# Loading float32 q and k with several tokens per row, and turning them head by head into stepped columns

## The chip, the core and the metric

The kernel runs on one core of a Trainium2 chip. The metric is the device time of one execution in microseconds. The core's engines work side by side, each through its own list of instructions in order: PE (matmuls, with its weight loads shown apart as PEld), DVE (vector), ACT (activation), POOL and SP. SP issues all DMAs here; they run on sixteen DMA engines.

## The reference

Attention with a decay, for 8 batches, 8 heads, 576 tokens and a head size of 64, followed by a feed-forward layer over all 4608 tokens:

```python
scores = scale * np.matmul(q, k.transpose(0, 1, 3, 2))
cum = np.cumsum(np.log(np.clip(f, 0.0001, 1.0)), axis=-1)
decay = cum[:, :, :, None] - cum[:, :, None, :]
scores = np.where(causal, -1000000000.0, scores + decay)
scores = scores - np.max(scores, axis=-1, keepdims=True)
attn = np.exp(scores)
attn = attn / (np.sum(attn, axis=-1, keepdims=True) + 1e-09)
out = np.matmul(attn, v)
...
h = x @ w_in          # x: out as (4608, 512); w_in: 512 x 2048
g = np.where(h >= 1, h, np.where(h <= -1, 0.0, (h + 1) ** 2 / 4))
return g @ w_out      # 2048 x 512
```

## The kernel before

Attention is cut into jobs. A job is one batch, one pair of heads and a range of blocks of 128 tokens (r0 to r1; the fifth block has 64 tokens). Batch 0 is cut in two, so jobs 0 to 3 are the four head pairs with token blocks 0 and 1, jobs 4 to 7 the same pairs with blocks 2 to 4 as queries and all five as keys; each later batch gives four jobs of five blocks. Jobs 0 to 11 (`NQK = 12`) compute q times k in float32; the later ones split q and k into two float16 parts and turn them with DMA transposes. Jobs 0 to 4 (`NPE = 5`) also keep the rest of attention in float32 on PE (`turn_rows`, L513 and L519, turns the probabilities; `early_values`, L544, multiplies them with v); from job 5 on the probabilities are split on ACT and DVE (L589, L595) and turned by DMA transposes (pT, L601 and L604).

`load` (L351, L355) fetches q and k of a job into one of two tiles, qk32_0 and qk32_1 (shown as qk_0 and qk_1), three jobs ahead. `early_prepare` turns them on PE (L388) into PSUM and copies them with ACT (L389) into a tile that has head size on the partitions and tokens along the row. `load_decay` (L362) loads a row of the running decay sums, cum_d, broadcast to all partitions, into one of three buffers called ck, once per job and head; a buffer is free again when POOL has used it for all token blocks of that head. `scores` multiplies q and k (L482) and lets POOL make the decay part from ck (L488) with its causal mask (L492); DVE adds the two and takes the minimum (L571), ACT takes the exponential (L575). The decay sums are computed at the start (f loaded, a scan on DVE, written to cum_d at L163).

The feed-forward weights are float32 blocks of 1024 KB, loaded by L201 into place (or into the tiles early and x1, shown as x) and then split: DVE turns the bits of each (L211, L214, L217), ACT takes the norm (L221) and the high part (L225), POOL (L227, L228) or DVE (L230) the low part. How many blocks are split in which job is set by the tables CONVERT and LOADS. When the first eight are done, DVE makes the scales early_z for the first units of the feed-forward layer, whose matmuls are L657 and L685. Units of it fill PE between the steps of attention, by a quota per job.

The order of the instructions on each engine isn't that of the source: a list scheduler orders them when the program is built, by its own model of when each is ready. A change of one part therefore moves others. SP too has one fixed order, and each DMA there also waits for the one issued eight DMAs earlier, whose semaphore it takes over.

Of the kernel before, what the change touches and what calls it, by code (L numbers as in the profile page):

```python
# [15 lines left out]
P = 128  # L16
# [15 lines left out]
NQK = 12  # L32
# [13 lines left out]
def kernel(  # L46
# [19 lines left out]
    nc = tc.nc  # L66

    B, H, S, D = q.shape
    DM, DF = w_in.shape
    NPAIR = H // 2  # L70
    NT5 = -(-S // P)
    LAST = NT5 - 1
    FULL = LAST * P
# [8 lines left out]
    ncut = NPAIR * sum(len(c) for c in CUTS.values())  # L82
# [60 lines left out]
    ident = const.tile([P, P], F32, name="ident")  # L143
# [186 lines left out]
    def load(ji):  # L330
        w = Pair()
        w.b, w.hp, w.r0, w.r1 = jobs[ji]
        w.p = ji
        w.sds = {}
        w.s0, w.s1 = P * w.r0, min(P * w.r1, S)
        w.cuts = [(w.s0, w.s1)] if w.s1 - w.s0 <= 512 else [(0, 64), (64, S)]
        h0 = 2 * w.hp
        flat = qk32[ji % 2].rearrange("p j h t d -> p (j h t d)")
        w.x32 = []
        for j, src in enumerate((q, k)):  # L340
            s_ = src[w.b, h0:h0 + 2]
            t0 = 0 if j else w.r0
            nt = w.r1 - t0
            x = flat[:, j * 2 * NT5 * D:j * 2 * NT5 * D + 2 * nt * D]
            w.x32.append(x)
            dst = x.rearrange("p (t h d) -> p h t d", t=nt, h=2)
            if NQK <= ji < max(NQK, ncut) + 2 and w.r1 == NT5:
                nc.gpsimd.memset(dst[64:P, :, nt - 1, :], 0.0)
            full = min(w.r1, LAST)
            for hh in range(2):  # L350
                nc.sync.dma_start(  # L351
                    dst[:, hh, 0:full - t0, :], s_[hh, P * t0:P * full, :].rearrange("(t p) d -> p t d", p=P)
                )
            if w.r1 == NT5:
                nc.sync.dma_start(dst[0:64, :, nt - 1, :], s_[:, FULL:S, :].rearrange("h p d -> p h d"))  # L355
        w.ck = []
        return w
# [17 lines left out]
    def early_prepare(w):  # L375

        t_ = early_qk[(w.p + NQK) % 2]
        w.nsig, w.nalpha = -8.0, -0.125
        bh = w.b * H + 2 * w.hp
        w.cqs = cq[:, :, bh:bh + 2]  # L380
        w.terms = ((t_[:, 0], t_[:, 1]),)
        for j in range(2):
            pt = ps.tile([P, 1024], F32, name="s")
            t0 = 0 if j else w.r0
            n = w.s1 - P * t0
            for c0 in range(0, n, P):
                m = min(P, n - c0)
                nc.tensor.transpose(pt[:, c0:c0 + m], w.x32[j][0:m, c0:c0 + P], ident[0:m, 0:m])  # L388
            nc.scalar.activation(t_[:, j, 0:n], pt[:, 0:n], AF.Copy)  # L389

    def measure(w):
# [17 lines left out]
    def prepare(w):  # L409
        if w.p < NQK:  # L410
            return early_prepare(w)
        sc = w.sc
        for j in range(2):
            nc.scalar.activation(qs[:, 2 * j], w.x32[j], AF.Copy, scale=sc[:, j:j + 1])  # L414
        for j in range(2):
            nc.vector.scalar_tensor_tensor(  # L416
                out=qs[:, 2 * j + 1], in0=w.x32[j], scalar=sc[:, j:j + 1], in1=qs[:, 2 * j],
                op0=ALU.mult, op1=ALU.subtract,
            )
        qkT = two.tile([P, 4, SP], F16, name="qkT")  # L420
        nc.sync.dma_start_transpose(
            qkT.rearrange("p c (b e) -> p (c b) e", e=P), qs.rearrange("p c e -> p (c e)")
        )
        qh, ql, kh, kl = (qkT[:, c] for c in range(4))
        w.terms = ((qh, kh), (ql, kh), (qh, kl))
# [309 lines left out]
    def weight_step():  # L735
# [6 lines left out]
        for first, end in groups:  # L742
            if nw == 2 * end:
                z = moe_scales(0, first, end - 1, True)
                for ch, e0, e1 in EARLY:
                    if (e0, e1) == (first, end):
                        for fb in range(first, end):
                            bsc[(ch, fb)] = z

    pairs = [load(0)]  # L750
    decay_sums()
    pairs.append(load(1))
    load_decay(pairs[0], 0)
    load_decay(pairs[0], 1)
# [3 lines left out]
    value_scale(0)  # L758
    split_values(pairs[0])
    pairs.append(load(2))  # L760
    for p in range(njobs + 1):
        w = pairs[p] if p < njobs else None
# [91 lines left out]
```

## Time and profile before

| | |
|---|---|
| median of three runs | 1116.96 us (1116.5 to 1118.39) |
| the profiled execution | 1118.56 us, span 1116.8 us |
| mean granted PE clock | 0.966 |
| PE, DVE, ACT, POOL busy | 91%, 72%, 71%, 38% |
| DMA packets | 408281, of them 383968 under 512 B |

The span is the time from the first to the last instruction of the profiled execution. Busy shares are means over the whole span; the stretch of the float32 jobs and of the weights, about the first quarter, looks different from the rest and is read by itself.

### The profile page before, as it was taken

How to read it: one execution, taken by the hardware profiler on the slowest of the kernel's cores; microseconds unless marked ns; L12 is line 12 of the kernel's file. 1: busy time of each engine (PE TensorE's matmuls, PEld its weight loads, DVE VectorE, ACT ScalarE, POOL GpSimd, SP SyncE). 2: the span in 40 equal slices, each digit the busy share in tenths (PEclk: the TensorE clock that was granted, in tenths of full speed). 3: DMA queues.
4: the chain of work that ended last, by engine and by line, in shares of the span. 5: the costliest groups of instructions: out<-in, count | busy, mean ns of one | idle time of the engine just before them, and what ended most of it. 6: DMA issues, size and time to landing. Idle time of an engine off the chain costs nothing. (4 is left out here: it accounts for less than half of the span.)

```text
span 1116.8 us, 24410 instructions
## 1 busy us (share of the span) xinstructions
PE 1017.8 (91%) x8811; PEld 663.8 (59%) x8811; DVE 799.0 (72%) x2095; ACT 790.0 (71%) x1638; POOL 427.4 (38%) x679
## 2 busy tenths in 40 slices
PE   4647789667999999999999999999999999999998
PEld 3424455335566666666766666566666666677665
DVE  4785987887989888887667668888888787322222
ACT  3665887756877887788667768787878887444443
POOL 3486665634544543343223324344343442000000
PEclk9968889778999999999999999999999999999999
DMA  7957765575978657766653666775776462200000
GB/s 235 303 143 222 167 147 125 142 191 116 190 172 166 159 143 170 167 152 148 118 140 78 155 119 153 168 174 139 166 167 155 116 124 73 66 21 1 19 20 19
DMA packets 408281, 152.18 MB, mean 136 GB/s; under 512 B 383968, under 2 KB 384992, under 8 KB 408160
## 3 DMA queue, kind: packets, MB, share of 16 engines
q1 hardware_dynamic: 408160, 150.63, 57.6%
q8 instruction: 69, 1.13, 0.4%
q14 instruction: 52, 0.43, 0.1%
HBM read 75.64 MB, written 9.58 MB: 76 GB/s over the span
## 5 line engine op out<-in xcount | busy, mean ns | idle before, releaser
L657 PE MATMUL ph<-x,place 128*128 128x256 f16 (+3 forms) x4608 | 413.3, 248 | 6.4 <-DVE u L668 5.5
L685 PE MATMUL po<-place,g 128*128 128x512 f16 x1728 | 401.9, 382 | 12.4 <-ACT g L670 8.2
L657 PEld LDWEIGHTS <-place 128*128 128x128 f16 x4608 | 354.1, 99 | 66.3 <-issue 18.0
L685 PEld LDWEIGHTS <-g 128*128 128x128 f16 x1728 | 166.4, 99 | 192.0 <-ACT g L670 10.5
L488 POOL TENSOR_SCALAR sdr<-ck,nsig,cqs 128x128 f32<-128x128 f32 (+1 forms) x192 | 145.8, 763 | 149.2 <-DVE pr L595 137.3
L575 ACT ACTIVATE sdr<-sdr,nm 128x384 f32<-128x384 f32 (+1 forms) x248 | 137.4, 554 | 66.9 <-DVE nm L571 57.0
L668 DVE SCALAR_TENSOR_TENSOR u<-ph,z,u 128x512 f32<-128x512 f32 x128 | 95.8, 748 | 113.1 <-ACT u L667 112.5
L488 POOL TENSOR_SCALAR sd<-ck,nsig,cqs 64x576 f32<-64x576 f32 x48 | 60.0, 1250 | 248.7 <-ACT qs L414 109.3
L666 ACT ACTIVATE u<-ph,z 128x512 f32<-128x512 f32 x128 | 97.9, 765 | 78.4 <-PE ph L657 78.4
L482 PE MATMUL s<-qkT 64*64 64x512 f16 (+11 forms) x1056 | 119.6, 342 | 34.1 <-DVE nm L571 30.6
L595 DVE SCALAR_TENSOR_TENSOR pr<-sdr,rc,pr 128x384 f16<-128x384 f32 (+2 forms) x232 | 130.5, 596 | 21.6 <-ACT pr L589 20.4
L670 ACT ACTIVATE g<-u,z 128x512 f16<-128x512 f32 x128 | 91.9, 718 | 67.6 <-DVE u L668 67.3
L671 DVE SCALAR_TENSOR_TENSOR g<-u,z,g 128x512 f16<-128x512 f32 x128 | 96.7, 756 | 47.2 <-ACT g L670 46.5
L589 ACT ACTIVATE pr<-sdr,rc 128x384 f16<-128x384 f32 (+1 forms) x236 | 119.3, 556 | 12.1 <-DVE rc L586 5.3
L571 DVE CUSTOM_DVE_ANT_0 sdr<-s,sdr,nalpha 128x128 f32<-128x128 f32 (+1 forms) x192 | 99.0, 545 | 13.1 <-PE s L482 8.3
L492 POOL TENSOR_SCALAR_AFFINE_SELECT sdr<-sdr 128x128 f32<-128x128 f32 x248 | 93.9, 389 | 9.7
L667 ACT ACTIVATE u<-u 128x512 f32<-128x512 f32 x144 | 89.5, 622 | 2.0
L615 PE MATMUL s<-pT,vs 128*64 128x320 f16 (+3 forms) x1098 | 70.9, 282 | 4.7 <-DVE nm L571 4.7
L615 PEld LDWEIGHTS <-vs 128*64 128x64 f16 x1098 | 49.7, 112 | 27.3 <-issue 8.8
L488 POOL TENSOR_SCALAR sdr<-ck,cq 128x384 f32<-128x384 f32 (+3 forms) x56 | 39.9, 712 | 66.2 <-DVE pr L595 38.3
L482 PEld LDWEIGHTS <-qkT 64*128 64x128 f16 (+1 forms) x864 | 33.8, 99 | 51.3 <-issue 35.9
L414 ACT ACTIVATE qs<-qk,sc 128x640 f16<-128x640 f32 x48 | 37.0, 818 | 22.4 <-DVE sc L140 22.4
(154 smaller groups left out, 1013.8 us busy)
## 6 DMA issues: line engine op xcount, KB each, us to landing
ck<-cum_d SPq DMA_DIRECT2D x64, 288.0 KB, 3.8
out_dram<-ot SPq DMA_DIRECT2D x36, 256.0 KB, 2.1
qk<-in_k_dram SPq DMA_DIRECT2D x64, 128.0 KB, 2.7
vst<-in_v_dram SPq DMA_DIRECT2D x28, 288.0 KB, 3.3
v<-in_v_dram SPq DMA_DIRECT2D x62, 128.0 KB, 2.6
qk<-in_q_dram SPq DMA_DIRECT2D x56, 128.0 KB, 2.7
place<-in_moe_w_in_dram SPq DMA_DIRECT2D x6, 1024.0 KB, 7.2
place<-in_moe_w_out_dram SPq DMA_DIRECT2D x5, 1024.0 KB, 7.2
```

What stands on the lines that cost most here:

```text
L482: nc.tensor.matmul(sds[h % len(sds)][1][p0:p1, c0:c1], lhsT=a[rows, q0 - w.s0:q0 - w.s0 + p1 - p0], rhs=b[rows, c0:c1], start=(i == 0), st ...
L488: nc.gpsimd.tensor_scalar(out=sd[p0:p1, 0:wid], in0=w.ck[h][p0:p1, 0:wid], scalar1=w.nsig if w.p < NQK else w.nsig[p0:p1], scalar2=w.cqs[p ...
L571: nc.vector.tensor_tensor_reduce(out=a, in0=sp[:, 0:wid], in1=a, scale=w.nalpha, scalar=BIG, op0=ALU.add, op1=ALU.min, accum_out=nm[:, i:i ...
L575: nc.scalar.activation(a, a, AF.Exp, bias=nm[:, i:i + 1], scale=-1.0, accum_out=sm[:, i:i + 1])
L589: nc.scalar.activation(pr[:, :, 0, i, :], a, AF.Copy, scale=rc[:, i:i + 1])
L595: nc.vector.scalar_tensor_tensor(out=pr[:, :, 1, i, :], in0=a, scalar=rc[:, i:i + 1], in1=pr[:, :, 0, i, :], op0=ALU.mult, op1=ALU.subtract,)
L615: nc.tensor.matmul(av[64 * h:64 * h + 64, at + s0:at + s1], lhsT=w.vs[:, vl, h, t, :], rhs=w.pT[:, t, pl, h, s0:s1], start=(t == 0 and pi ...
L657: nc.tensor.matmul(ph[:, fi, a0:a1], lhsT=wi[fb][:, wl, t, fi * P:(fi + 1) * P], rhs=xs[b][:, t, xl, s0:s0 + a1 - a0], start=(fi == 0 and ...
L666: nc.scalar.activation(u, h, AF.Relu, scale=z.u[:, i:i + 1], bias=z.h[:, i:i + 1])
L668: nc.vector.scalar_tensor_tensor(out=u, in0=h, scalar=z.t[:, i:i + 1], in1=u, op0=ALU.max, op1=ALU.min)
L671: nc.vector.scalar_tensor_tensor(out=g[:, 1], in0=u, scalar=z.r[:, i:i + 1], in1=g[:, 0], op0=ALU.mult, op1=ALU.subtract)
L685: nc.tensor.matmul(po[ch][i], lhsT=g[:, gl, fi * TC + i * P:fi * TC + (i + 1) * P], rhs=wo[fb][:, wl, fi, :], start=(first and fi == 0 and ...
```

## The change

For jobs 0 to 11, partition p of q and k holds n neighbouring tokens (n is 2 or 4, the number of full blocks loaded) in place of tokens p, 128 + p and so on. A row of a partition is then one run of 512 or 1024 B instead of n runs of 256 B, and both heads come in one DMA in place of two. The fifth block's 64 tokens are loaded as before. Since neighbouring tokens now stand in one partition, a turned block no longer gives 128 neighbouring columns: each head's 128 x 64 piece is multiplied with the identity on PE, and its result goes to every n-th column of the 64 partitions of its head. Each transpose of a full block (128 partitions, two heads side by side) becomes two matmuls with 64 output partitions. A zero fill in `load` is untouched for the later jobs; its condition is only written shorter.

```diff
+            full = min(w.r1, LAST)
+            if ji < NQK:
+                n = full - t0
+                nc.sync.dma_start(
+                    x[:, 0:2 * n * D].rearrange("p (h e) -> p h e", h=2),
+                    s_[:, P * t0:P * full, :].rearrange("h (p n) d -> p h (n d)", p=P),
+                )
+                if w.r1 == NT5:
+                    tail = x[0:64, 2 * n * D:2 * nt * D].rearrange("p (h d) -> p h d", h=2)
+                    nc.sync.dma_start(tail, s_[:, FULL:S, :].rearrange("h p d -> p h d"))
+                continue
             dst = x.rearrange("p (t h d) -> p h t d", t=nt, h=2)
-            if NQK <= ji < max(NQK, ncut) + 2 and w.r1 == NT5:
+            if ji < max(NQK, ncut) + 2 and w.r1 == NT5:
                 nc.gpsimd.memset(dst[64:P, :, nt - 1, :], 0.0)
-            full = min(w.r1, LAST)
...
             n = w.s1 - P * t0
-            for c0 in range(0, n, P):
-                m = min(P, n - c0)
-                nc.tensor.transpose(pt[:, c0:c0 + m], w.x32[j][0:m, c0:c0 + P], ident[0:m, 0:m])
+            g = min(w.r1, LAST) - t0
+            rows = w.x32[j][:, 0:2 * g * D].rearrange("p (h n d) -> p h n d", h=2, n=g)
+            cols = pt[:, 0:g * P].rearrange("c (p n) -> c n p", n=g)
+            for i in range(g):
+                for h in range(2):
+                    nc.tensor.matmul(cols[64 * h:64 * h + 64, i], lhsT=rows[:, h, i], rhs=ident, start=True, stop=True)
+            if w.r1 == NT5:
+                nc.tensor.transpose(pt[:, g * P:n], w.x32[j][0:64, 2 * g * D:2 * (g + 1) * D], ident[0:64, 0:64])
             nc.scalar.activation(t_[:, j, 0:n], pt[:, 0:n], AF.Copy)
```

Lines of the changed kernel stand 10 lower behind the first edit and 15 lower behind the second (L362 becomes L372, L488 becomes L503, L571 becomes L586); the loads of q and k are L349 and L355 there.

The scheduler's order moves with it. On SP, around the write of cum_d at the start, there stood before (x<-in_v_dram are pieces of v for its scale, vs<-in_v_dram is v of a job):

```order
L163 DMA cum_d<-x 64x576
L250 DMA x<-in_v_dram 128x576 x2
L440 DMA vs<-in_v_dram 128x2x64
L362 DMA ck<-cum_d 128x256 x2
L440 DMA vs<-in_v_dram 128x2x64
L351 DMA qk_0_98<-in_q_dram 128x2x64 x2
L351 DMA qk_0_98<-in_k_dram 128x2x64 x2
L362 DMA ck<-cum_d 128x256
L201 DMA place<-in_moe_w_in_dram 128x4x512
L201 DMA place<-in_moe_w_out_dram 128x2x1024
L201 DMA place<-in_moe_w_in_dram 128x4x512
L362 DMA ck<-cum_d 128x256
```

The pieces of v now go ahead of the write, and behind it stand:

```order
L163 DMA cum_d<-x 64x576
L201 DMA place<-in_moe_w_in_dram 128x4x512
L201 DMA place<-in_moe_w_out_dram 128x2x1024
L349 DMA qk_0_98<-in_q_dram 128x2x128
L201 DMA place<-in_moe_w_in_dram 128x4x512
L372 DMA ck<-cum_d 128x256 x2
L349 DMA qk_0_98<-in_k_dram 128x2x128
L372 DMA ck<-cum_d 128x256
L455 DMA vs<-in_v_dram 128x2x64 x2
```

The first two ck (job 0) have moved behind three weight blocks. The fourth ck (job 1, second head) stood in the last row of the first list, behind three weight blocks; now it is the one in this later piece of SP's row, behind nine:

```order
L201 DMA place<-in_moe_w_out_dram 128x2x1024
L201 DMA place<-in_moe_w_in_dram 128x4x512
L201 DMA place<-in_moe_w_out_dram 128x2x1024
L355 DMA qk_0_98<-in_q_dram 64x2x64
L355 DMA qk_0_98<-in_k_dram 64x2x64
L201 DMA place<-in_moe_w_in_dram 128x4x512
L201 DMA x<-in_moe_w_out_dram 128x2x1024
L355 DMA qk_1_99<-in_q_dram 64x2x64
L355 DMA qk_1_99<-in_k_dram 64x2x64
L201 DMA x<-in_moe_w_out_dram 128x2x1024
L455 DMA v_100<-in_v_dram 128x4x64 x2
L372 DMA ck<-cum_d 128x256
```

On DVE, at the first step of job 4 (sdr_101 with 128x384), there stood before, behind six split weight blocks and in the seventh:

```order
L217 SCALAR_TENSOR_TENSOR place<-place,qs 128x1024
L211 TENSOR_SCALAR qs<-place 128x1024
L230 SCALAR_TENSOR_TENSOR place<-place,sw 128x1024
L214 SCALAR_TENSOR_TENSOR qs<-place,qs 128x1024
L132 TENSOR_SCALAR mp<-ph 128x2
L448 SCALAR_TENSOR_TENSOR vs<-v_100,sv,vs 128x640
L552 SCALAR_TENSOR_TENSOR x<-po_726,sv,x 128x256
L571 ISA sdr_101,nm<-s,sdr_101 128x384
```

Now, behind three split blocks (L217 here ends the third):

```order
L567 SCALAR_TENSOR_TENSOR x<-po_580,sv,x 128x256
L593 TENSOR_SCALAR rc<-sm_542 128x2
L217 SCALAR_TENSOR_TENSOR place<-place,qs 128x1024
L594 RECIPROCAL rc<-rc 128x2
L586 ISA sdr_101,nm<-s,sdr_101 128x384
L586 ISA nm 128x1
L586 ISA sdr_102,nm<-s,sdr_102 128x384
L586 ISA nm 128x1
L211 TENSOR_SCALAR qs<-place 128x1024
```

Job 4's steps have moved ahead of the fourth weight block on DVE. From some way into the jobs with float16 parts on, all engines have the order of before.

## The prediction

> **What bounds the kernel now.** I read the page's engine shares and the forty slices first, then the windows of 28 us over the first third, then the waits there, and last the timelines of SP, POOL and DVE.
>
> ```profile
> PE 1017.8 (91%) x8811; PEld 663.8 (59%) x8811; DVE 799.0 (72%) x2095; ACT 790.0 (71%) x1638; POOL 427.4 (38%) x679
> ...
> DVE  4785987887989888887667668888888787322222
> ...
> DMA  7957765575978657766653666775776462200000
> ```
>
> ```profile
> 56.00:84.00 28.00, 13.03 (x57) 7.56 (x55) 24.11 (x52) 18.89 (x37) 22.40 (x20) 0.68 0.56 145
> ...
> 308.00:336.00 28.00, 28.00 (x344) 19.34 (x339) 23.11 (x57) 21.11 (x46) 13.96 (x20) 1.00 0.70 166
> 336.00:364.00 28.00, 28.00 (x272) 18.33 (x269) 25.40 (x83) 22.58 (x49) 11.18 (x21) 1.00 0.81 174
> sum 364.00, PE 275.45 PEld 172.94 DVE 288.08 ACT 256.27 POOL 195.73; mean PE 21.19 PEld 13.30 DVE 22.16 ACT 19.71 POOL 15.06
> ```
>
> In the windows the five busy times are PE, PEld, DVE, ACT, POOL, then the granted clock, the DMA share and GB/s. PE is idle for 1116.8 - 1017.8 = 99.0 us in all. From 308 us on its windows are full; before that it works 275.45 - 56.00 = 219.5 of 308, so 88.5 us of its idle time lie in the first 308 us. The matmuls still to come are the same, so what the change does to that first stretch, where the float32 jobs run, is carried to the end. There DVE is the fullest engine (24.11 of 28 us in 56:84), with POOL close behind (22.40).
>
> ```profile
> POOL sdr L488 <- DMA ck<-cum_d: 14.8, 3, 7.7
> POOL sd L488 <- DMA ck<-cum_d: 14.4, 3, 10.3
> POOL pr L488 <- DMA ck<-cum_d: 8.3, 3, 6.7
> ACT qkT L389 <- PE s L388: 10.5, 7, 3.6
> ```
>
> These waits are total, times and longest, over the first 300 us. POOL waits 37.5 us there for the broadcast decay rows ck, ACT 10.5 us for the transposes of q and k.
>
> **The change part by part.** First the packets.
>
> ```profile
> DMA packets 2304, 0.84 MB, mean 195 GB/s; under 512 B 2172, under 2 KB 2172, under 8 KB 2304
> ...
> q1 hardware_dynamic: 2304, 0.84, 80.2%
> ```
>
> ```profile
> DMA packets 2585, 2.38 MB, mean 298 GB/s; under 512 B 1687, under 2 KB 1894, under 8 KB 2585
> ...
> q1 hardware_dynamic: 2585, 2.38, 92.3%
> ```
>
> ```profile
> DMA packets 3170, 3.82 MB, mean 319 GB/s; under 512 B 1950, under 2 KB 2127, under 8 KB 3168
> ...
> ck<-cum_d SPq DMA_DIRECT2D x1, 128.0 KB, 11.1
> ```
>
> The first answer is 110.2 to 114.5 us, nearly all 256 B rows: 0.802 x 16 x 4.3 us / 2304 = 24 ns a packet. The second is 20 to 28 us: 0.923 x 16 x 8 us = 118 us, less 1687 x 24 ns, leaves 87 ns for each of 898 packets of some 2.2 KB. The trace has no q or k row of 512 B or 1 KB; their packets cost between 24 ns (size is free) and 48 and 96 ns (no gain). On the line between the two measured sizes I take 32 and 49 ns. A pair of rows then saves 16 ns, four save 47. Jobs 0 to 3 have 512 pairs (8 us over 16 engines, 0.5 us each); jobs 4 to 7 256 pairs and 256 fours (1.0 us); jobs 8 to 11 512 fours (1.5 us): 12 us of full DMA time, between 0 and 18. Only the 4 us of jobs 0 to 5 fall where DMA is nearly full (92.3% above); later work hides most of the rest.
>
> ```profile
> L351 SPq DMA_DIRECT2D qk<-in_q_dram x72: 368/498/1925, 2.5 to 855.3; - x72
> ```
>
> 24 issues fall away (two for each of 12 jobs), at a median of 0.50 us: 12 us of SP's queue, behind which ck, v and the DMA transposes of pT stand.
>
> Now PE. 88 transposes become 16 (the 64-row tails) and 144 matmuls of 64 output partitions in 72 pairs.
>
> ```profile
> L388 PE MATMUL s<-ident,qk 128*128 128x128 f32 x48 | 12.5, 393 | 8.6 <-DVE nm L571 6.0 <-ACT qkT L389 2.6
> L513 PE MATMUL ph<-pr,sdr 128*128 128x128 f32 x52 | 11.0, 386 | 1.2 <-ACT pr L502 1.2
> ```
>
> ```profile
> 23.72 1.55 PE L544 MATMUL po<-pT,vs 128*64 128x256 f32 x8 [0.69 <-ACT pT L524]
> 28.47 1.11 PE L388 MATMUL s<-ident,qk 128*128 128x128 f32 x4 [3.20 <-DVE nm L571]
> ...
> 99.05 2.42 PE L544 MATMUL s<-pT,vs 128*64 128x320 f32 x20
> ...
> 103.90 0.86 PE L388 MATMUL s<-ident,qk 128*128 128x128 f32 x5 [1.86 <-ACT qkT L389]
> ```
>
> L544 has the shape of the new ones: 64 columns, the two heads in alternate halves, and longer rows. It takes 0.19 us each early and 0.12 us at 99 us, a pair 0.39 and 0.24; a transpose takes 0.28 and 0.17. So a pair costs 0.07 to 0.11 us more: 5 to 8 us in 72 pairs, 0 if the halves overlap fully, 20 if each costs a whole early transpose. Nothing shows what a stepped PSUM write costs; I take it as free, and keep the 20 as the bound. The 88.5 us of idle PE cover most; ACT's wait for L388 shows that some is exposed. I take 1.0 us (0 to 10). Against the change speaks a rule of the Trainium skill, "TensorE: Matmul & The Clock Gate", section Terms: its transpose mode is four times faster for FP32. By it a pair would cost some eight transposes, an estimate of 90 to 140 us of PE in all; the rows do not bear it out, since L388 at 393 ns lies beside the full float32 matmuls of L513 at 386 ns. The sum goes by the rows.
>
> The largest term is the order. With fewer q and k issues, SP reaches the weights sooner, and the ck rows come after them.
>
> ```profile
> 7.38 0.49 SPq L163 DMA_DIRECT2D cum_d<-x  x1
> ...
> 9.74 0.81 SPq L362 DMA_DIRECT2D ck<-cum_d  x2
> ```
>
> ```profile
> 13.51 1.42 POOL L488 TENSOR_SCALAR sdr<-ck,cq 128x128 f32<-128x128 f32 x3 [7.75 <-DMA ck<-cum_d]
> ...
> 26.28 1.44 POOL L488 TENSOR_SCALAR pr<-ck,cq 128x128 f32<-128x128 f32 x2 [6.69 <-DMA ck<-cum_d]
> ```
>
> ```profile
> 26.20:76.10 49.90, 31.17 (x36) 0.90 0.79 231
> ```
>
> ```profile
> L228 POOL TENSOR_TENSOR place<-place 128x1024 f16<-128x1024 f32 x2 | 4.8, 2410 | 0.0
> L227 POOL TENSOR_SCALAR place<-place,sw 128x1024 f32<-128x1024 f32 x2 | 3.1, 1566 | 0.2 <-ACT place L225 0.2
> ```
>
> Before, job 0's ck land at 13.51 and the fourth ck (job 1, second head) at 26.28. Now three weight loads stand ahead of the first ck; a ck that stood behind three took 11.1 us to land (the row above), against some 3.8 from 9.74 to 13.51, so job 0 starts about 5 us later. The fourth stands behind nine of 1.05 MB. With all that SP issues first this is 13.1 MB; at the 319 GB/s of 28 to 40 us, counted from 2 us, it lands at 43; at the 400 GB/s of packets of 2.2 KB and 87 ns alone, at 35. I take 40, since the rows of 256 B to 1 KB between the weights pull towards the mean. Then POOL must make the decay tiles of job 1's second head and of jobs 2, 3 and 4 before DVE's first step of job 4, which now stands ahead of the fourth weight block: POOL's busy time from 26.2 to 76.1, 31.2 us, less one low part of a weight block that now comes later ((4.8 + 3.1) / 2 = 4), is 27 us. DVE's first step of job 4 comes at 40 + 27 = 67.
>
> ```profile
> 62.58 1.55 DVE L211 TENSOR_SCALAR qs<-place 128x1024 int32<-128x1024 int32 x1
> ...
> 68.21 0.54 DVE L571 CUSTOM_DVE_ANT_0 sdr<-s,sdr 128x384 f32<-128x384 f32 x1
> ...
> 90.88 0.56 DVE L571 CUSTOM_DVE_ANT_0 sdr<-s,sdr 128x384 f32<-128x384 f32 x1 [3.76 <-POOL sdr L492]
> ```
>
> ```profile
> L217 DVE SCALAR_TENSOR_TENSOR place<-place,qs 128x1024 int32<-128x1024 int32 x7 | 9.4, 1337 | 0.0
> L214 DVE SCALAR_TENSOR_TENSOR qs<-place,qs 128x1024 int32<-128x1024 int32 x7 | 8.9, 1274 | 0.0
> L211 DVE TENSOR_SCALAR qs<-place 128x1024 int32<-128x1024 int32 x7 | 7.6, 1087 | 0.0
> ```
>
> ```profile
> 64.00:87.10 23.10, 9.85 (x38) 6.10 (x40) 18.39 (x50) 14.61 (x29) 20.21 (x19) 0.56 0.51 152
> 91.00:109.00 18.00, 14.79 (x89) 8.84 (x90) 10.24 (x26) 12.31 (x26) 11.17 (x19) 0.91 0.72 187
> ```
>
> That is where job 4 began before, too (68.21), but then six weight blocks had been turned (the seventh began at 62.58), now three. Three blocks cost 3 x (9.4 + 8.9 + 7.6) / 7 = 11.1 us of DVE. With the 18.4 us that DVE worked from 64 to 87.1 this is 29.5: the weight group ends at 67 + 29.5 = 96.5, not 87.1. What DVE waited there before (4.7 of 23.1 us) is gone, as its data are in. Job 5's first step follows at 97, not 90.9: 6 us late. From 91 to 109 us DVE had 18 - 10.2 = 7.8 us of idle time; I let half of it be taken up. That leaves 6 - 3.9 = 2.1 us (between 0, all of it taken, and 6, none). Later DMA and SP savings I count with 0.3 us: ACT and DVE had other work during most of POOL's waits for ck.
>
> The sum: 2.1 (order) + 1.0 (PE) - 0.3 (DMA, SP) = +2.8 us. The profiled execution took 1118.56 us, 1.6 above the median of the three runs, so it becomes 1121.4, and the median 1116.96 + 2.8 = 1119.8. A measurement tells from no change what differs by over 0.2%, 2.2 us.
>
> **The rivals.** No change: the 7.8 us of DVE idle time after 91 take up all of the delay, or the fourth ck lands at 35 and job 4 starts at 62, five us sooner than taken; about 1117. For it speaks that those 7.8 us are nearly half of the stretch; against it that DVE, POOL and SP each take their steps in one fixed order, so that a late one holds up all behind it.
>
> Faster: from 84 us on, the loads of jobs 8 to 11 take 1.5 us less of DMA each and half the issues, so the ck that POOL waited 14.4 us for in three places (10.3 in one) come earlier. If a third of that stood on the path, 4.8 us go, and with the start at no loss it is 1112.5. It decides if those three waits fall under 5 us together. Against it: DVE works 288 of the first 364 us (the sum row above), so that much of what comes earlier waits for DVE.
>
> PE: a pair costs a whole 0.56 us (no overlap, or a slow stepped write), 20 us in all, and half shows: 1127. It would show as pairs of over 0.45 us. L544 speaks against it. The Trainium skill's rule on transposes (same page and section), by its estimate of 90 to 140 us and the same half, would give some 1160 to 1190; I hold that for 1 in 100, inside this case.
>
> **How the numbers follow.** The late ck rows 0.38 (1119.3 to 1124), no change 0.27, faster 0.28, PE 0.07. So faster 0.28, same 0.27, slower 0.45. The range from 1111.0 to 1125.0 takes in the faster case and the late ck with no idle time taken up, and leaves out the PE case and a little on each side.
>
> **What would show it.** In the changed profile: fewer, larger packets for q and k at 27 to 54 ns; the first POOL decay row at about 18 to 19 us; the one of job 1's second head near 40; DVE's first 128x384 step near 67, and job 5's near 97; pairs on PE at 0.24 to 0.39 us. The prediction is wrong if the fourth ck lands before 35, if POOL needs much under 27 us from there, or if DVE's idle time from 91 to 290 us shrinks by more than 3 us.

## The result, and the profile after

The changed kernel is slower: 1133.04 us median (1131.08 to 1133.95, four runs) against 1117.68 (1116.5 to 1118.69, four runs) for the kernel before; the ratio is 1.0135, with a 95% interval of 1.0118 to 1.0153. Forecast were 1119.8 us and a range up to 1125.0. The sign was right; 15 us were lost where 2.8 were expected.

The page of the changed kernel (the span, the busy shares, DVE in forty slices):

```profile
span 1131.2 us, 24812 instructions
...
PE 1025.1 (91%) x9027; PEld 670.2 (59%) x9027; DVE 802.1 (71%) x2095; ACT 790.6 (70%) x1638; POOL 418.1 (37%) x679
...
DVE  3487877888988888887678668888888887322232
```

DVE does the same work as before (802.1 against 799.0 us), but its first slices are emptier: 3 4 8 7 where there were 4 7 8 5. The windows say it in microseconds. The columns are the length, then PE, PEld, DVE, ACT and POOL busy, the granted clock, the DMA share and GB/s. First before, then after:

```profile
0.00:112.00 112.00, 65.56 (x310) 41.96 (x310) 72.00 (x174) 64.34 (x145) 63.97 (x95) 0.89 0.77 226
112.00:196.00 84.00, 68.34 (x494) 42.49 (x495) 71.83 (x182) 67.92 (x140) 51.47 (x71) 0.92 0.65 145
```

```profile
0.00:112.00 112.00, 61.65 (x390) 42.82 (x392) 64.59 (x161) 59.18 (x137) 48.27 (x83) 0.71 0.64 210
112.00:196.00 84.00, 67.39 (x512) 41.13 (x508) 68.25 (x165) 62.40 (x128) 54.14 (x70) 0.92 0.60 149
```

At 112 us DVE is 7.4 us of work behind, at 196 us 11.0. Most of it is lost in one window, before and after:

```profile
28.00:56.00 28.00, 18.24 (x77) 12.44 (x78) 21.09 (x51) 19.23 (x52) 13.70 (x20) 1.00 0.95 303
```

```profile
28.00:56.00 28.00, 15.80 (x110) 11.98 (x112) 12.55 (x36) 15.05 (x40) 8.17 (x23) 0.66 0.83 258
```

What DVE waits for from 20 to 68 us (total, times, longest), before and after:

```profile
DVE sdr L571 <- POOL sdr L492: 2.8, 2, 1.8
DVE pr L571 <- POOL pr L492: 2.1, 3, 1.2
```

```profile
DVE sdr L586 <- POOL sdr L507: 12.5, 3, 6.8
...
DVE pr L586 <- POOL pr L507: 3.9, 2, 3.7
```

It waits 16.4 us there for POOL's decay tiles, where it waited 4.9. POOL itself waits for ck (timeline of POOL after; the second row is job 1's second head):

```profile
19.71 1.99 POOL L503 TENSOR_SCALAR sdr<-ck,cq 128x128 f32<-128x128 f32 x4 [13.95 <-DMA ck<-cum_d]
...
41.49 0.94 POOL L503 TENSOR_SCALAR pr<-ck,cq 128x128 f32<-128x128 f32 x2 [17.05 <-DMA ck<-cum_d]
```

And the ck wait on SP (its queue after): two weight loads go out ahead of q, a third ahead of the first ck, and the fourth ck is issued at 34.23, behind nine.

```profile
7.38 0.48 SPq L163 DMA_DIRECT2D cum_d<-x  x1
7.91 0.59 SPq L201 DMA_DIRECT2D place<-in_moe_w_in_dram  x1
8.54 0.57 SPq L201 DMA_DIRECT2D place<-in_moe_w_out_dram  x1
...
10.67 1.38 SPq L372 DMA_DIRECT2D ck<-cum_d  x2
...
34.23 2.43 SPq L372 DMA_DIRECT2D ck<-cum_d  x1
```

The delay grows and then stays. A job's values are computed while the next job runs; I name the place by that next job, as the expectations do. Their first matmul (L615 before, L630 after) comes at 117.6 and 123.9 us in job 6 (+6.3), at 167.9 and 178.0 in job 8 (+10.1), at 214.2 and 227.7 in job 10 (+13.6), at 414.7 and 429.6 in job 17 (+14.8). What is missing then is work of PE: by 364 us it has done 768 matmul records of the feed-forward layer's first product (L672), where it had done 826 (L657).

### The profile page after: what moved, and what is told of

Its sections match the earlier page's. It is cut to its first block, busy times and chain, and to the rows that moved or that the text cites. A ratio compares the mean times of both kernels' runs of the same rounds, so it can differ in the third digit from the quotient of the medians.

```text
span 1131.2 us, 24812 instructions
## 1 busy us (share of the span) xinstructions
PE 1025.1 (91%) x9027; PEld 670.2 (59%) x9027; DVE 802.1 (71%) x2095; ACT 790.6 (70%) x1638; POOL 418.1 (37%) x679
## 5 line engine op out<-in xcount | busy, mean ns | idle before, releaser
L672 PE MATMUL ph<-x,place 128*128 128x256 f16 (+3 forms) x4608 | 414.7, 249 | 9.4 <-DVE u L683 5.4
L672 PEld LDWEIGHTS <-place 128*128 128x128 f16 x4608 | 354.2, 99 | 69.9 <-issue 23.2
L503 POOL TENSOR_SCALAR sdr<-ck,nsig,cqs 128x128 f32<-128x128 f32 (+1 forms) x192 | 150.0, 784 | 149.2 <-DVE pr L610 134.6
L503 POOL TENSOR_SCALAR sd<-ck,nsig,cqs 64x576 f32<-64x576 f32 x48 | 57.2, 1193 | 253.5 <-ACT qs L429 109.2
L604 ACT ACTIVATE pr<-sdr,rc 128x384 f16<-128x384 f32 (+1 forms) x236 | 119.2, 556 | 12.8 <-DVE rc L601 6.3
L586 DVE CUSTOM_DVE_ANT_0 sdr<-s,sdr,nalpha 128x128 f32<-128x128 f32 (+1 forms) x192 | 98.9, 544 | 10.2 <-PE s L497 6.6
L507 POOL TENSOR_SCALAR_AFFINE_SELECT sdr<-sdr 128x128 f32<-128x128 f32 x248 | 85.3, 355 | 9.5
L630 PE MATMUL s<-pT,vs 128*64 128x320 f16 (+3 forms) x1098 | 70.4, 280 | 5.1 <-DVE nm L586 4.5
L630 PEld LDWEIGHTS <-vs 128*64 128x64 f16 x1098 | 49.3, 111 | 28.0 <-issue 11.1
L503 POOL TENSOR_SCALAR sdr<-ck,cq 128x384 f32<-128x384 f32 (+3 forms) x56 | 42.3, 755 | 59.2 <-DVE pr L610 24.7
```

The lines of the kernel that those rows point to most:

```text
L503: nc.gpsimd.tensor_scalar(out=sd[p0:p1, 0:wid], in0=w.ck[h][p0:p1, 0:wid], scalar1=w.nsig if w.p < NQK else w.nsig[p0:p1], scalar2=w.cqs[p ...
L586: nc.vector.tensor_tensor_reduce(out=a, in0=sp[:, 0:wid], in1=a, scale=w.nalpha, scalar=BIG, op0=ALU.add, op1=ALU.min, accum_out=nm[:, i:i ...
L604: nc.scalar.activation(pr[:, :, 0, i, :], a, AF.Copy, scale=rc[:, i:i + 1])
L630: nc.tensor.matmul(av[64 * h:64 * h + 64, at + s0:at + s1], lhsT=w.vs[:, vl, h, t, :], rhs=w.pT[:, t, pl, h, s0:s1], start=(t == 0 and pi ...
L672: nc.tensor.matmul(ph[:, fi, a0:a1], lhsT=wi[fb][:, wl, t, fi * P:(fi + 1) * P], rhs=xs[b][:, t, xl, s0:s0 + a1 - a0], start=(fi == 0 and ...
```

## The experiments

Theory A: the order of ck and weights costs the time, and layout, packets and matmuls cost nearly nothing. Theory B: the matmuls on PE cost it. Theory C: A is true of the start, and the order inside jobs 6 to 9 has a cause of its own.

**The new rows with one transfer for each head**

```diff
-                nc.sync.dma_start(x[:, 0:2 * n * D]..., s_[:, P * t0:P * full, :]...)   # both heads
+                for hh in range(2):
+                    nc.sync.dma_start(x[:, hh * n * D:(hh + 1) * n * D],
+                                      s_[hh, P * t0:P * full, :].rearrange("(p n) d -> p (n d)", p=P))
```

> The new rows and the new matmuls, but one transfer for each head, so that SP has as many q and k issues as before; its first 24 issues then stand in the order of before, with the first two ck ahead of all weights. Theory A (the order: ck behind the weights): the first decay row on POOL at 13 to 14 us again, job 1's second-head row near 26, the total 1114 to 1119 us, 0.997 to 1.001 of before. Theory B (the 144 matmuls of 64 columns on PE cost it): 1128 to 1134, as the changed kernel. Theory C (half early ck, half the order of jobs 6 to 9, which has its own cause): 1122 to 1127.

Measured: 1122.57 us, ratio 1.0044 (1.0030 to 1.0058). The first decay row came at 13.66 us. With the issues of before the scheduler keeps the SP order of before, and two thirds of the loss are gone: B is out as the main cause. What is left, 5 us, lies in the range of C and above that of A; the same kernel with earlier weight blocks, below, bears on it.

**The whole change, with the weights behind the ck**

```diff
-        nc.sync.dma_start(raw(n)..., src)
+        in_order(nc.sync.dma_start(raw(n)..., src))   # behind the SP issue that stands ahead of it in the program
```

> The whole change, and each weight load held behind the SP issue that stands ahead of it in the program, so that the first three ck go out ahead of every weight and the fourth behind three. Theory A: first decay row on POOL before 16 us, job 1's second-head row before 30, the total 1112 to 1119 us. Theory B (PE): 1128 to 1134. Theory C (both heads in one transfer are themselves late, since a k that is awaited comes with twice the bytes): 1121 to 1127.

Measured: 1115.90 us, ratio 0.9989 (0.9976 to 1.0002). POOL's rows, and the first window:

```profile
13.86 0.95 POOL L503 TENSOR_SCALAR sdr<-ck,cq 128x128 f32<-128x128 f32 x2 [8.10 <-DMA ck<-cum_d]
...
26.10 0.95 POOL L503 TENSOR_SCALAR pr<-ck,cq 128x128 f32<-128x128 f32 x2 [6.44 <-DMA ck<-cum_d]
```

```profile
0.00:112.00 112.00, 76.78 (x461) 52.64 (x463) 79.46 (x186) 67.72 (x155) 63.82 (x98) 0.73 0.72 227
```

The ck are back where they were (13.5 and 26.3 before), both heads still come in one transfer, and nothing is lost. The mean granted clock in this window is 0.73, nearly the 0.71 of the changed kernel, so it isn't the clock that costs the time.

**The matmuls alone**, on the loads of before, into plain columns

```diff
-                nc.tensor.transpose(pt[:, c0:c0 + m], w.x32[j][0:m, c0:c0 + P], ident[0:m, 0:m])
+                for h in range(2):      # full blocks; the 64-row tails stay transposes
+                    nc.tensor.matmul(pt[64 * h:64 * h + 64, c0:c0 + P],
+                                     lhsT=w.x32[j][:, c0 + 64 * h:c0 + 64 * h + 64], rhs=ident, start=True, stop=True)
```

> The kernel before with its loads as they were, and each full transpose of q and k replaced by two matmuls of 64 columns, one for each head, into plain (not stepped) columns. Theory A: 1115 to 1119 us, since the pairs overlap and take what a transpose took (0.28 us early, 0.17 late). Theory B: 1124 to 1133, with pairs of 0.39 us or more.

Measured: 1119.31 us, ratio 1.0018 (1.0005 to 1.0031), at most 3.5 us: a little above A's range, far under B's. The pair does not cost what a transpose costs, though; that part of the expectation was a miscount, taken up below.

**The order alone**, on the loads and transposes of before

```diff
+        with tc.issue_after(issue.ins):     # behind the store of cum_d
+            load_weights(3)
...
+        load_weights({3: 8}.get(2 * w.p + h, 0))    # five more ahead of the fourth ck
+        if 2 * w.p + h in (0, 3):
+            in_order(issue)                  # the ck load
```

> The kernel before, loads and transposes as they were, with three weight loads issued right behind the store of cum_d and five more ahead of the fourth ck, as the changed kernel has them. Theory A: first decay row near 19 us, job 1's second-head row at 38 to 42, the total 1126 to 1134 us. Theory B: 1115 to 1119. Theory C (the start-up alone costs some 6 to 8 us, the rest comes with the order of jobs 6 to 9): 1122 to 1126.

Measured: 1129.96 us, ratio 1.0112 (1.0090 to 1.0134). POOL:

```profile
20.80 1.42 POOL L493 TENSOR_SCALAR sdr<-ck,cq 128x128 f32<-128x128 f32 x3 [15.03 <-DMA ck<-cum_d]
...
40.01 0.94 POOL L493 TENSOR_SCALAR pr<-ck,cq 128x128 f32<-128x128 f32 x2 [13.36 <-DMA ck<-cum_d]
```

Not a byte of q or k is loaded otherwise, and 12 of the 15 us are there. With the second experiment this shows A from both sides.

**The four ck of jobs 0 and 1 issued by ACT**

```diff
-        nc.sync.dma_start(
+        (nc.scalar if w.p < 2 else nc.sync).dma_start(
             ck[:, 0:w.s1], cum_d[bh...
```

> The whole change, with the four ck of jobs 0 and 1 issued by ACT instead of SP; the weights still go out as early on SP as in the changed kernel, and DVE keeps its order there (four weight blocks ahead of job 4's first step). Theory A1 (it is the wait of ck in SP's queue that costs): job 1's second-head row on POOL by 28 us, job 4's first 128x384 step by 62, the total 1114 to 1121 us. Theory A2 (it is the weights in flight: ck waits for DMA engines whoever issues it): first row at 17 to 20, job 1's second-head row at 36 or later, the total 1126 to 1133. Theory D (DVE's order, job 4's first step ahead of the last four weight blocks, costs by itself): early rows, but job 5's first step still at 96 or later and the total 1123 to 1129.

Measured: 1135.17 us, ratio 1.0145 (1.0120 to 1.0169): no better, and above the range of every theory. ACT's timeline:

```profile
14.04 0.66 ACT L404 ACTIVATE qkT<-s 128x256 f32<-128x256 f32 x2 [2.67 <-DMA place<-in_moe_w_in_dram]
35.99 0.33 ACTq L372 DMA_DIRECT2D ck<-cum_d  x1
36.34 1.28 ACT L590 ACT_TABLE_LOAD   x1 [21.64 <-DMA place<-in_moe_w_in_dram]
```

From 14.7 to 36.0 us ACT does nothing: by the profile its fourth ck waits for a weight load that SP issued earlier, and everything on ACT stands behind that issue. The bypass moved the wait from SP, which computes nothing, to an engine that does. The first row came at 17.63, only 2 us sooner, although the ck was issued at 9.91, right behind three weight loads: that speaks for A2, the weights in flight, for the first row; the fourth, held up with ACT, tells nothing.

**Jobs 6 and 7 held behind their weight blocks** on DVE

```diff
+            if w.p in (6, 7) and r == w.r0 and i == 0:
+                in_order(step)       # the first tensor_tensor_reduce of the job
```

> The changed kernel, with DVE's first step of job 6 held behind weight block 10 and that of job 7 behind block 12 (counted from 1); in the changed kernel both blocks are turned later, in the midst of these jobs. Theory C (the late ck cost 6 to 8 us, the rest is the order in jobs 6 to 9): job 6's values still about 6 us later than before, job 10's no more than 9 later, the total 1124 to 1128 us. Theory A (all follows from the start): 1130 to 1134.

Measured: 1148.04 us, ratio 1.0259 (1.0238 to 1.0280). No theory gave that. On DVE between block 10 and job 6:

```profile
130.32 0.16 DVE L132 TENSOR_SCALAR mp<-ph 128x2 f32<-128x2 f32 x1 [1.94 <-PE ph L131]
...
133.47 1.29 DVE L230 SCALAR_TENSOR_TENSOR place<-place,sw 128x1024 f16<-128x1024 f32 x1 [2.38 <-ACT place L225]
136.89 0.75 DVE L685 SCALAR_TENSOR_TENSOR u<-ph,early_z,u 128x512 f32<-128x512 f32 x1 [2.13 <-ACT u L684]
...
139.10 0.55 DVE L586 CUSTOM_DVE_ANT_0 sdr<-s,sdr 128x384 f32<-128x384 f32 x1
```

A block is a chain DVE, ACT, PE, DVE, ACT, DVE. Interleaved with a job's steps its gaps are filled; pinned in one piece they stand open, and job 6's first step moves from 119.3 to 139.1 us. In that time DVE works 10.3 us here, and 17.7 in the changed kernel. The experiment says nothing about C: it added a cost of its own.

**Weight blocks earlier, ck still late**

```diff
-CONVERT = {1: 1, 2: 1, 3: 2, 5: 1, ...
+CONVERT = {0: 1, 1: 1, 2: 1, 3: 1, 5: 1, ...
```

> The changed kernel with the ck as late as there, but the second pair of weight blocks turned during job 1 and the third during job 2, that is in the time in which DVE waits for the late rows (the table CONVERT has one pair each at jobs 0, 1, 2 and 3). If DVE's idle time between 28 and 56 us (15.5 us, before 6.9) is the loss, 7 us of weight work move into it: job 5's first step near 94, the total 1122 to 1127 us. If the loss is POOL's late start and DVE's work doesn't matter: job 5's first step at 100, the total 1130 to 1135.

Measured: 1119.74 us, ratio 1.0009 (0.9995 to 1.0023): the whole loss is gone, more than was expected, with the first decay row still at 19.81 us.

```profile
0.00:112.00 112.00, 63.04 (x419) 44.22 (x420) 71.31 (x173) 63.66 (x145) 56.67 (x95) 0.74 0.71 225
112.00:196.00 84.00, 72.42 (x582) 44.20 (x580) 71.18 (x179) 66.33 (x137) 49.03 (x66) 0.94 0.63 142
```

DVE has done 142.5 us of work by 196 us, before 143.8. So a late ck need not cost anything, if weight work is done while it is awaited. The table moves each block's steps on ACT and POOL along with those on DVE; that DVE's share is the one that counts is argued here, not shown. The values in job 6 were 11.0 us late, later than in the changed kernel, and those in job 12 0.9 us early: how late a job starts is no measure of the loss. DVE's work done by 196 us is a better one.

**Both orders held** (second and sixth experiment together)

> The whole change, the weight loads held behind the ck as in the second run, and DVE's first steps of jobs 6 and 7 held behind weight blocks 10 and 12. That run was 7.0 us ahead of the kernel before at job 6's values and 1.2 us ahead at the end. Theory C (the order in jobs 6 to 9 gave it back): 1109 to 1114 us. If DVE or PE is full there whatever the order: 1114 to 1118.

Measured: 1127.83 us, ratio 1.0080 (1.0061 to 1.0099). The pins cost 10 us here, 14 in the sixth (by the ratios); the time lies above both ranges.

**Two controls on the kernel before.** The table CONVERT of the seventh experiment, and the `in_order` of the second, each as the only edit.

> A control for the run with the earlier weight blocks: the kernel before, loads and transposes as they were, with only the table CONVERT changed (one pair of weight blocks each at jobs 0, 1, 2 and 3). If the earlier blocks helped the changed kernel by filling the time in which DVE waits for the late ck, there is less to fill here (DVE idles 6.9 of the 28 us from 28 on): within 0.4% of before, 1113 to 1121 us. If the earlier blocks are a gain of their own, whatever the ck do: 1102 to 1110 us, and then that run showed nothing about the ck.

> A control for the second run: the kernel before, with its weight loads held behind the SP issue that stands ahead of them in the program. Its first 30 SP issues stay as they were. If that run was no slower than before because the ck went first: 1114 to 1119 us here. If holding the weights is a gain of its own, which hid a cost of the layout: 1104 to 1111.

Measured: 1117.75 us, ratio 1.0009 (0.9991 to 1.0027), and 1119.21 us, ratio 1.0013 (1.0000 to 1.0026). The second is just above its range. Neither edit is a gain of its own, so both experiments took away a loss rather than covering it.

**Two versions that might have beaten both**: the second and seventh experiment together, and the first with the earlier weight blocks.

> The whole change, with the ck ahead of the weights and the earlier weight blocks together, as a version that might beat both. If DVE's idle time up to 200 us sets the end: DVE busy 79 of the first 112 us or more, 1108 to 1114 us. If the gain at the start is again given back in jobs 6 to 9 (7.0 us ahead at job 6, 1.2 at the end in the second run): 1114 to 1118.

> New rows and matmuls with one transfer for each head (before's SP order) and the earlier weight blocks. That kernel without them was 0.44% slower than before, its job 4's first step having moved ahead of the seventh weight block. If it was this order on DVE: 1114 to 1119 us here. If the new rows or matmuls cost it: 1121 to 1125.

Measured: 1116.90 us, ratio 0.9998 (0.9986 to 1.0010), and 1118.98 us, ratio 1.0009 (0.9997 to 1.0022). Neither beats the kernel before. The second is in the range expected if what the first experiment had left (1.0044) was the order on DVE too.

**Weight blocks later, on the kernel before**

```diff
-CONVERT = {1: 1, 2: 1, 3: 2, 5: 1, ...
+CONVERT = {1: 1, 3: 3, 5: 1, ...
```

> The kernel before, loads, ck and transposes as they were, with the second pair of weight blocks moved from job 2 to job 3 (the table CONVERT alone), so that DVE has turned five blocks and not seven when job 4's first step comes. If weight work that DVE puts off behind job 4 is what the late ck cost (theory A, in this form): two blocks, 2 x 3.7 = 7.4 us, carried to the end whole or more, 1122 to 1130 us. If the late ck cost through POOL or ACT: 1115 to 1119.

Measured: 1121.61 us, ratio 1.0042 (1.0024 to 1.0060), just under the range. The ck are early (26.22 us for the fourth), and DVE is short of work where it was in the changed kernel:

```profile
28.00:56.00 28.00, 18.59 (x82) 12.36 (x82) 16.19 (x44) 17.61 (x48) 9.83 (x18) 0.56 0.89 288
```

4.9 us less than before in this window, and 4.7 us lost at the end. So the order of the weight blocks costs time by itself, without late ck, packets or matmuls. But missing work in this window isn't enough to tell the loss. By 112 us DVE was level with before here (72.74 against 72.00), and the seventh experiment's kernel worked no more in the window and lost nothing (this kernel, then that one):

```profile
0.00:112.00 112.00, 67.09 (x293) 42.82 (x294) 72.74 (x170) 64.43 (x145) 55.87 (x89) 0.68 0.71 215
```

```profile
28.00:56.00 28.00, 13.96 (x104) 10.59 (x102) 16.73 (x45) 17.34 (x41) 12.08 (x24) 0.66 0.73 233
```

**The wait at 160 us.** In the changed kernel DVE waits once for 3.5 us in the stretch where +6 becomes +14 (waits of DVE, 112 to 196 us):

```profile
DVE mp L132 <- PE ph L131: 3.5, 1, 3.5
```

The trace leads from there to PE, ACT and POOL's low part of a weight block. Two runs moved a low part to DVE (`if n % 2 == 0 and n != 10`, then `n != 8`, at POOL's branch of `weight_split`).

> The changed kernel, with the low part of the eleventh weight block computed by DVE instead of POOL. In the changed kernel POOL ends that low part at 157.9 us and DVE's next weight scales wait 3.52 us for it, by way of ACT and PE, at 160.9. If that wait is passed on to the end (a half of what is added after job 6): 1128 to 1131 us, job 10's values some 3 us earlier. If it is taken up behind it: 1132 to 1134.

> The changed kernel, with the low part of the ninth weight block (not the eleventh, as in the run before: the ninth one's bits lie in the place that the eleventh block's squares overwrite, and that is what ACT waits for until 157.9 us) computed by DVE instead of POOL. If that wait is a half of what is added after job 6: no DVE wait of 3.5 us at the weight scales near 160, the total 1127 to 1131 us. If it is taken up by the waits behind it: 1132 to 1135.

The first took the wrong block: the wait stood at 3.5 us, 1131.08 us, ratio 1.0115 (1.0084 to 1.0147). In the second the wait was shorter:

```profile
DVE mp L132 <- PE ph L131: 1.5, 1, 1.5
```

and the time 1130.01 us, ratio 1.0105 (1.0087 to 1.0122). Against the changed kernel's 1.0135 (1.0118 to 1.0153) the intervals still touch, and the run that removed nothing measured 1.0115. That this wait is a part of the growth is likely and not shown.

**All of them in one table**, DVE's busy time up to 196 us (the sum of the two windows, in the one profiled execution) beside the ratio of all runs:

| kernel | DVE busy to 196 us | ratio |
|---|---|---|
| jobs 6 and 7 pinned | 126.2 | 1.0259 |
| ck from ACT | 128.4 | 1.0145 |
| low part, wrong block | 130.9 | 1.0115 |
| the change | 132.8 | 1.0135 |
| the order alone | 136.4 | 1.0112 |
| low part, right block | 137.9 | 1.0105 |
| both orders held | 138.2 | 1.0080 |
| two transfers | 140.7 | 1.0044 |
| matmuls alone | 142.1 | 1.0018 |
| before, blocks later | 142.2 | 1.0042 |
| the change, blocks earlier | 142.5 | 1.0009 |
| two transfers, blocks earlier | 143.4 | 1.0009 |
| before, weights held | 143.5 | 1.0013 |
| before | 143.8 | 1 |
| before, blocks earlier | 144.6 | 1.0009 |
| the change, weights held, blocks earlier | 146.1 | 0.9998 |
| the change, weights held | 150.7 | 0.9989 |

Where DVE is more than 5 us behind, each microsecond of it goes with one to two at the end (15.4 with 16 for ck from ACT, 11.0 with 15 for the change, 5.9 with 12 for the low part of the right block). Near 142 the sum no longer tells the kernels apart: 1.6 us behind go with 4.7 for the later blocks, 1.3 with 1.0 for the change with earlier ones. PE's records of L657 (L672) by 364 us do for these two: 797 and 827, against 826 before. Above 144 us 7 more bring 1.2, which the interval doesn't separate from nothing. What holds the time there was not tried.

## Why the prediction was right and wrong

**Right: what moves, and the way.** The SP order, with the weights ahead of the ck, was named as the largest term, and its places came out: the first decay row at 19.71 us (18 to 19 forecast), job 1's second head at 41.49 (near 40), DVE's first step of job 4 at 67.10 (67). The fourth experiment shows that this order by itself costs 12 us. The 67 was in part luck: the prediction took POOL to work 27 us from the fourth ck on, and POOL worked 18.5 of the 25.6 us and waited for the rest. Much less than 27 was one of the prediction's own signs of being wrong.

```profile
41.49:67.10 25.61, 17.47 (x134) 12.18 (x134) 11.26 (x42) 17.05 (x48) 18.47 (x34) 0.77 0.56 150
```

**Wrong: the size of the delay.** "The weight group ends at 67 + 29.5 = 96.5", job 5's first step at 97. DVE after:

```profile
67.10 0.56 DVE L586 CUSTOM_DVE_ANT_0 sdr<-s,sdr 128x384 f32<-128x384 f32 x1 [4.71 <-POOL sdr L507]
...
97.99 2.01 DVE L230 SCALAR_TENSOR_TENSOR place<-x,sw,place 128x1024 f16<-128x1024 f32 x1
100.85 0.56 DVE L586 CUSTOM_DVE_ANT_0 sdr<-s,sdr 128x384 f32<-128x384 f32 x1 [0.85 <-POOL sdr L507]
```

The group ended at 100.0 and job 5 began 10.0 us late, not 6. DVE's gaps were gone, as the sum had it; the work in it was too small:

```profile
67.10:100.00 32.90, 20.77 (x106) 14.55 (x107) 31.73 (x63) 22.69 (x41) 14.57 (x12) 0.63 0.20 54
```

DVE worked 31.7 us there where the sum had 29.5, and was idle for 1.2 in the group and 0.85 behind it. Two small steps of early_z (L289 and L312) took 3.0 us together, and 0.4 before; what slowed them the traces don't show.

**Wrong, and the step that failed: "I let half of it be taken up".** This step made 2.1 us of the order, the term that measured 12 by itself (fourth experiment). The half was even right at first, by luck: 10.0 us at job 5's first step were 6.3 at the values in job 6. But from there the delay grew again, by 7.3 us up to job 10. The idle time of one stretch (7.8 us from 91 to 109) was read as room in which a delay vanishes. From 91 to 290 us, where the prediction feared that DVE's idle time would shrink, it grew from 35.0 to 37.1 us (the 199 us less the third busy time; before, then after):

```profile
91.00:290.00 199.00, 152.24 (x1044) 90.33 (x1044) 164.01 (x452) 145.36 (x305) 108.21 (x154) 0.86 0.66 153
```

```profile
91.00:290.00 199.00, 152.32 (x1094) 92.13 (x1095) 161.86 (x446) 139.24 (x288) 110.50 (x147) 0.89 0.61 155
```

So none of that idle time was used to catch up. Of DVE's work 8.5 us were not done from 28 to 56 us, while it waited for the late ck; 7.4 were still missing at 112 us and 11.0 at 196, and by 364 us, when PE is full, it had worked 277 us and not 288. The prediction priced when job 5 starts, and not how much work is left. The seventh experiment shows that the first doesn't decide; that DVE's work left does is likely from the table above, and not shown apart.

**Wrong in size, small in effect: PE.** The pair was taken at 0.24 to 0.39 us from L544. A float32 matmul leaves two records in this trace and a transpose one: 144 new matmuls are 288 records, and L544's eight records were four matmuls. After, and before:

```profile
L401 PE MATMUL s<-ident,qk 128*64 128x128 f32 x288 | 26.5, 334 | 27.5 <-DVE nm L586 24.4 <-DVE x L640 2.3 <-ACT qkT L404 0.6
...
24.10 1.97 PE L401 MATMUL s<-ident,qk 128*64 128x128 f32 x16 [9.82 <-DVE nm L586]
```

```profile
L388 PE MATMUL s<-ident,qk 128*128 128x128 f32 x72 | 16.2, 355 | 11.4 <-DVE nm L571 7.7 <-ACT qkT L389 3.7
```

Job 2's four pairs take 1.97 us, 0.49 each, where four transposes took 1.11 (28.47, in the prediction); the granted clock was 0.50 from 23 to 26 us after and 1.00 from 28 to 30 before. Other pairs take from 0.27 us (four in 1.09 at 51.45) to 0.56 (two in 1.12 at 70.31). Over all 72 a pair took 0.37 us and a transpose 0.23. PE has 10.3 us more, above the 5 to 8 forecast, and the mark of the PE rival (over 0.45 us a pair) was met by many pairs. Its price was not: alone, with everything else as before, the matmuls cost 0.6 to 3.5 us (third experiment), where the sum had 1.0. There PE works 12.8 us more than before and is idle for 12.2 less (86.8 against 99.0), so most of them run while PE would wait. The page "TensorE: Matmul & The Clock Gate" of the Trainium skill (Terms) says that the transpose mode is four times faster for FP32; the prediction put that aside because L388 and L513 take the same time for a record. With two records for a matmul, for those of L513 too, a full one took 0.77 us there against 0.39 for a transpose, and a pair of 64 columns costs 1.6 transposes over all: the rule had the direction, the trace shows a factor of about two and not four.

**Small, and a half of it wrong: packets.** From 2 to 8 us, before and after (packets and bytes; the queue's share of the 16 engines):

```profile
DMA packets 2544, 1.26 MB, mean 210 GB/s; under 512 B 2224, under 2 KB 2224, under 8 KB 2544
...
q1 hardware_dynamic: 2544, 1.26, 79.1%
```

```profile
DMA packets 1698, 1.75 MB, mean 291 GB/s; under 512 B 148, under 2 KB 1169, under 8 KB 1698
...
q1 hardware_dynamic: 1698, 1.75, 94.2%
```

Before, 0.791 x 16 x 6 = 75.9 us less 320 packets of 2.3 KB at 87 ns leave 21.6 ns for one of 256 B. After, 90.4 us less 529 x 87 ns and 148 x 24 ns leave 40 ns for one of 512 B, an estimate, since the 87 ns come from another stretch. By it a pair of rows saves 3 ns as one packet, not the 16 that the line between 24 and 87 ns gave. The page "DMA: Bandwidth & Descriptors" of the Trainium skill (Specifications) puts the least transfer for the full rate at 512 B; here 512 B in 40 ns are 12.8 B a ns and 2.3 KB in 87 ns are 26, so the trace does not agree.

**The rivals.** No change is what the layout does in the four kernels whose ck go first or whose weight blocks are split earlier (0.9989 to 1.0009), but the idle time that was to bring it did not. The faster rival looked to POOL's waits of 14.4 us for ck (sd tiles, up to 300 us). They came to 13.6 in the changed kernel and fell to 5.1 in the second experiment, near the mark of 5, and even there the time did not fall by more than the interval allows for no change.

**What stays open**: why 7.4 us of missing DVE work at 112 us have become 11.0 at 196. One wait of 3.5 us is a candidate. With the order alone (fourth experiment) the values in job 6 were already 12.0 us late and those in job 17 7.9, and with the later blocks (thirteenth) 6.2 and 6.3. So neither of the two orders alone shows the growth, and theory C, that the order in jobs 6 to 9 has a cause of its own, isn't settled.

## What to carry to other kernels

Where a scheduler orders the queues, fewer issues are an edit of the order. Look at what now goes out ahead of the first small load on which the start hangs. Ask of a delay not how late the next stage begins but which engine has to catch up, and how much of its work is left; idle time further on is room only if that work can be done there. A late load can be made harmless by giving the waiting engine other work (here a table of four numbers), and a wait on a DMA should stay on a queue that no computing engine shares.

## What the runs showed of the hardware that was not expected

A DMA issue placed on ACT held up ACT's computation for 21.6 us, since by the profile the issue itself waited for another DMA. A packet of 512 B took about 40 ns by the estimate above, almost twice one of 256 B (21.6 ns), and less than half of one of 2.3 KB (87 ns). Two float32 matmuls of 64 columns, four records, took 0.37 us in the mean of 72 pairs where a float32 transpose took 0.23.
